# One tile for bank 6 of PSUM in an attention and DFT kernel: value sums and scores share it, and every value product has 17 columns

## The chip, the cores and the metric

The kernel runs on one core of a Trainium2 chip. Its time is device microseconds (us) from the run's own measurement; a kernel's time is the median of several runs. The profile is one further execution with the hardware profiler on; its span goes from the first to the last instruction, and is a little shorter than the time measured for that same execution.

## The reference

Two mixers work on sequences of 2048 rows and 512 columns, and a gate adds them. The first is a Fourier mix, written as products with DFT matrices; the second is softmax attention with 32 heads of 16 columns.

```python
def _A_ref(x, dft_seq_re, dft_seq_im, dft_hid_re, dft_hid_im):
    a = jnp.einsum("bsd,ed->bse", x, dft_hid_re)
    b = jnp.einsum("bsd,ed->bse", x, dft_hid_im)
    return jnp.einsum("ts,bse->bte", dft_seq_re, a) - jnp.einsum("ts,bse->bte", dft_seq_im, b)

def _B_ref(x, wqkv, wo):
    ...
    scores = jnp.einsum("bhqd,bhkd->bhqk", q, k) * scale
    p = _softmax(scores, axis=-1)
    o = jnp.einsum("bhqk,bhkd->bhqd", p, v)
    return (lambda x, *d: x.transpose(*d))(o, 0, 2, 1, 3).reshape(B, S, D) @ wo

g = _sigmoid((x * gate_w).sum(-1, keepdims=True))
return g * a + (1 - g) * b
```

## The kernel before

Everything is written out in the order in which each engine is to run it; no scheduler moves it. The attention goes by pairs of heads (16 pairs), halves of the queries (2) and blocks of 128 keys (16): 512 units in all. For each unit, four score products of 128 keys by 512 queries (line 795, two query blocks, two heads) go to PSUM, ScalarE (ACT in the profile) takes their exponential into an SBUF tile `pt` (line 796), and a value product for each of the four multiplies the exponentials with the values (line 843). Scores need the row maxima first, so each score tile is also computed a first time with queries and keys swapped (line 292, kind "a" below), and VectorE (DVE) takes the maximum of it (line 294). Scores of kind "s" are those of line 795.

A score or maximum product uses 64 of TensorE's 128 rows. Beside it, on the other 64 rows, runs half of a DFT or projection product (line 469). A value product uses all 128 rows and one 32-column quarter of the array; the four of a unit stand in the four quarters and run side by side. Each is one matmul in the program, with single-precision operands; the profile shows it as two matmuls, each with a weight load of its own. So a unit has two groups of four matmuls in the profile.

A value product has 17 stationary columns: 16 value columns and a column of ones, which gives the sum that the softmax divides by. It writes partitions 32j to 32j+16 of bank 6, for j from 0 to 3. The rest of each quarter is never used, but the copies out of the bank take all 128 partitions.

PSUM has eight banks. Scores use banks 0 to 6 by number, the DFT and projection chains use the eighth. Bank 6 is shared: value products add up in it (the tile `acc`), and between two sums it takes scores too. The order of the middle of the kernel is written as strings of slots, played by `segment`. The one that holds most of the time is

```python
FULL = "a5 s4 a2 s0 a3 s6 a5 s4 s1 s0 s2 a6 a3 a4 s5 a1 | |"
```

A letter with a digit is a product of that kind in that bank; each also issues one line-469 matmul on the other half of the rows. A bar is the value products of one unit. The last bar of a segment closes the sum: `evacuate` has ACT copy bank 6 to SBUF (line 822, or line 816 for the first copy of a total), and GpSimd (POOL) adds it to the running total (line 823). So in `FULL` bank 6 goes through: the copy of the last sum, the score `s6`, its exponential on ACT, the maximum product `a6`, its maximum on DVE, the value products of two units, the copy. There are 192 `FULL` segments; 26 `THIN` and 26 `NINE` segments have two bars with other slots between them and use bank 6 for an `s6` alone; with the opening at the start that is 245 sums.

Before the change each use of bank 6 by a score is a tile of its own (`s` or `a`) of a pool with one buffer, and each sum opens with a new tile `acc`. A new tile in that buffer waits for the end of all use of the last. Because the copy reads all 128 partitions of a tile that is new, the first value products of a sum are 32 columns wide (`width`), so that they write each partition of their quarter; the columns past the 17th are values of another head, and what they give is not used.

Of the kernel before, what the change touches and what calls it, by code (L numbers as in the profile page):

```python
# [9 lines left out]
F32 = mybir.dt.float32  # L10
# [5 lines left out]
P = 128  # L16
# [6 lines left out]
NT = S // P  # L23
# [8 lines left out]
def mix_kernel(ctx: ExitStack, tc: tile.TileContext, xa_t, xa, wqkv, w_hid, w_seq, wo, gate_w, out):  # L32
# [5 lines left out]
    nc = tc.nc  # L38
# [29 lines left out]
    psO = Ring(6)  # L68
# [31 lines left out]
    acc = psO.tile([P, 512], F32, "acc")  # L100
# [86 lines left out]
    def bank():  # L187
        nonlocal banks
        banks += 1
        return (psS if banks % 2 else psA).tile([P, 512], F32, name="s" if banks % 2 else "a")  # L190


    with tc.tile_pool(name="qk", bufs=1, reuse_waits="tile") as pool:
# [38 lines left out]
        for tb in range(4):  # L232
# [4 lines left out]
            for c in range(2):  # L237
                if tb == 0 and c == 0:
                    pss = [bank() for _ in range(4)]
                    for kt in range(KT):  # L240
                        x = xab[tb][:, :, :, kt * P:(kt + 1) * P]
# [8 lines left out]
                for ct in range(4):  # L250
                    ps = bank()
# [34 lines left out]
    def a_tile(i, h, ps=None, bank=None):  # L286
        p, j = divmod(i, 64)
        qt, kb = divmod(j, 4)
        if ps is None:
            ps = psA.tile([P, 512], F32, "a", bank)  # L290
        r = slice(64 * h, 64 * h + (64 if p else 48))
        nc.tensor.matmul(ps, qs[p % 2][r, qt * P:(qt + 1) * P], ks[p % 2][r, kb * 512:(kb + 1) * 512],  # L292
                         start=True, stop=True)
        user = nc.vector.tensor_reduce(mx[p % 2][:, h, qt, kb:kb + 1], ps, AX.X, ALU.max)  # L294
        hf = j // 32
        a_left[p, hf] = a_left.get((p, hf), 64) - 1
        if not a_left[p, hf]:
            deferred.extend((partial(m_parts, p, hf), partial(m_rows, p, hf)))
        return user
# [111 lines left out]
    for s in range(8):  # L411
        ps = psS.tile([P, 512], F32, name="s")
# [369 lines left out]
    def scores(u, qb, h, bank=(psS, "s"), number=None):  # L782
        p, r = divmod(u, 32)
        hf, kt = divmod(r, 16)
        q0 = hf * 1024 + qb * 512
        if u >= UNITS - 16:

            blk, kt = divmod(kt, 8)
            q0, kt = 1024 + blk * 512, 2 * kt + qb
        if u not in pts:  # L790
            pts[u] = work.tile([P, 4, 512], F32, name="pt", bufs=4)
        pool, name = bank
        ps = pool.tile([P, 512], F32, name=name) if number is None else pool.tile([P, 512], F32, name, number)
        rr = slice(64 * h, 64 * h + (64 if p else 50))
        nc.tensor.matmul(ps, ks[p % 2][rr, kt * P:(kt + 1) * P], qs[p % 2][rr, q0:q0 + 512], start=True, stop=True)  # L795
        return nc.scalar.activation(pts[u][:, 2 * qb + h], ps, AF.Exp, bias=0.0, scale=DH ** -0.5)  # L796

    def pv_last(u):
        blk, k2 = divmod(u - UNITS + 16, 8)
        pt = pts.pop(u)  # L800
        for j in range(4):
            x, h = divmod(j, 2)
            nc.tensor.matmul(acc[32 * j:32 * j + 17], vt[:, 2 * k2 + x, NP - 1, 16 * h:16 * h + 17], pt[:, j],
                             start=k2 == 0, stop=k2 == 7)
        if blk == 0 and k2 == 7:
            last_pairs.append(LastPair(0, [(psS, "s"), (psA, "a")]))
            last_pairs[0].copy(1)

    part = []

    def evacuate(p, hf, done):

        nonlocal total
        if total is None:
            total = work.tile([P, 512], F32, name="oe", bufs=2)
            nc.scalar.copy(total, acc)
        else:
            if not part:
                two = work.tile([P, 2, 512], F32, name="part", tag="w15")
                part.extend(two[:, i] for i in range(2))  # L820
            part.reverse()
            nc.scalar.copy(part[0], acc)  # L822
            nc.gpsimd.tensor_tensor(total, total, part[0], ALU.add)  # L823
        if done:
            for qb in range(2):
                nc.sync.dma_start(o_d[hf][p, :, qb * 512:(qb + 1) * 512], total[64 * qb:64 * qb + 64])
            total = None

    def pv(u, close=False):
        nonlocal acc  # L830
        if u >= UNITS - 16:
            return pv_last(u)
        p, r = divmod(u, 32)
        hf, kt = divmod(r, 16)
        pt = pts.pop(u)
        begin, done, width = acc is None or kt == 0, kt == NT - 1, 17
        if acc is None:
            acc = psO.tile([P, 512], F32, "acc")
            width = 32
        v = vt.rearrange("p t n d -> p (t n d)")[:, 33 * (NP * kt + p):]  # L840
        for j in range(4):
            h = j % 2
            i = nc.tensor.matmul(acc[32 * j:32 * j + width], v[:, 16 * h:16 * h + width], pt[:, j],  # L843
                                 start=begin, stop=done or close)
        if done or close:
            evacuate(p, hf, done)
            if close:
                acc = None
        return i

    def take(gen, n, whole=True):
# [84 lines left out]
    users, valued, exponentials = [], 0, []  # L936

    def score(kind, h, number=None):
        x = next(streams[h][kind == "a"], None)
        if x:  # L940
            users.append((kind, a_tile(*x, bank=number) if kind == "a" else scores(*x, number=number)))
            if kind == "s":
                exponentials.append(users[-1][1])

    def values(close=False):
        nonlocal valued
        i = pv(valued, close)
        valued += 1
        return i

    def segment(pattern, half, ds, stop):
# [6 lines left out]
        for n, slot in enumerate(pattern.split()):  # L958
# [18 lines left out]
            if first:  # L977

                score(slot, 1 - half, number)
# [12 lines left out]
            if slot != "-" and not first:  # L992
                score(slot[-1] if slot[0] == "+" else slot[0], 1 - half, number)
            if len(slot) == 2 and slot[0] != "+":
                score(slot[1].lower(), half, other)
# [38 lines left out]
    for bank in (*three[:1], *three):  # L1034
        scores(*next(streams[1][0]), bank)
# [8 lines left out]
    for u in range(valued + 2, UNITS, 2):  # L1044
        run_plan(u)
        for i in range(4):
            if i == 2:
                for gen, n in whole[u]:
                    pump(gen, n)
                if u == 506:  # L1050
                    last_pairs[0].turn()
                elif u == 508:
                    last_pairs[0].back()
            for h in range(2):
                scores(u + i // 2, i % 2, h, three[h])
        values()
        values()
    last_pairs[0].products([(psS, "s"), (psA, "a"), (psA, "a"), (psD, "d")], range(4))
    pv(UNITS - 2)
    pv(UNITS - 1)  # L1060
    last_pair(late)

# [35 lines left out]
```

## Time and profile before

| | |
|---|---|
| median of 3 runs | 1665.3 us (1664.87 to 1665.42) |
| the profiled execution's own time | 1664.94 us |
| its span | 1663.0 us |
| mean granted TensorE clock | 0.999 |
| PE (TensorE matmul) busy | 1655.0 us |
| PEld (TensorE weight load) busy | 1008.6 us |
| DVE, ACT, POOL busy | 1382.6, 1266.0, 653.5 us |

A row of the profile that groups instructions reads: line, engine, operation, what it writes and reads, shapes, and count; then the busy time in us, the mean of one in ns, and the engine's idle time just before, with what ended it. A form such as `128*32` is active rows by active columns. Matmuls overlap, so their busy time is a union, and the end of each is modelled. In a timeline a row is a start in us, a length in us, the engine and the instruction.

### The profile page before, as it was taken

To read this page: it belongs to the slowest core of one execution; us is meant where nothing else is said; L and a number is where in the kernel's file an instruction comes from. 1 tells how busy PE (TensorE), PEld (TensorE's weight loads), DVE (VectorE), ACT (ScalarE), POOL (GpSimd) and SP (SyncE) were. 2 spreads that over 40 slices of the span, in tenths; PEclk is the share of its full clock that TensorE was granted. 3 is DMA by queue.
4 is the path that set the end of the run, shared out by engine and by line. 5 is a ranking of instruction groups with operands and counts; after the bars stand their busy time and mean duration, and the time that the engine had idled before them with its cause. 6 is when DMAs were issued, how large, how long until landed. Compare 5 with 4: busy or idle time off the path is not lost.

```text
span 1663.0 us, 34370 instructions
## 1 busy us (share of the span) xinstructions
PE 1655.0 (100%) x13040; PEld 1008.6 (61%) x13040; DVE 1382.6 (83%) x2361; ACT 1266.0 (76%) x2469; POOL 653.5 (39%) x615
## 2 busy tenths in 40 slices
PE   9999999999999999999999999999999999999998
PEld 7888855556566656665666656665566556644443
DVE  5439888888888888888888888888888888899954
ACT  5212388888888888888788888888788878889996
POOL 0202133443434455444343455544444456333330
PEclk9999999999999999999999999999999999999999
DMA  9973610414151343414157534315141535462114
GB/s 295 349 158 120 180 15 9 70 34 85 44 93 47 73 112 81 94 46 79 47 90 254 93 114 96 88 56 90 52 85 59 112 103 122 139 188 40 37 32 140
DMA packets 85245, 167.13 MB, mean 100 GB/s; under 512 B 22461, under 2 KB 22717, under 8 KB 81069
## 3 DMA queue, kind: packets, MB, share of 16 engines
q1 hardware_dynamic: 84648, 164.30, 39.5%
q8 instruction: 102, 1.67, 0.5%
q10 hardware_dynamic: 432, 0.66, 0.1%
q14 instruction: 63, 0.51, 0.1%
HBM read 109.67 MB, written 55.17 MB: 99 GB/s over the span
## 4 chain that ended last, share of the span: by engine, by line
PE 98%; DMA 1%; DVE 0%; POOL 0%; SPq 0%; issue 0%; DVEq 0%; ACT 0%; POOLq 0%; ACTq 0%
PE acc L843 28%; PE d L469 24%; PE a L292 17%; PE s L795 16%; PE s L383 3%; PE s L415 1%; PE d L383 1%; PE a L108 1%; PE s L108 1%; PE s L107 1%; PE a L107 1%; PE a L109 1%; PE s L109 1%; PE a L469 1%; PE s L469 0%; PE s L244 0%
## 5 line engine op out<-in xcount | busy, mean ns | idle before, releaser
L294 DVE TENSOR_REDUCE mx<-a 128x1 f32<-128x512 f32 x2026 | 1260.1, 683 | 172.8 <-PE a L292 144.5
L796 ACT ACTIVATE pt<-s 128x512 f32<-128x512 f32 x2006 | 1021.9, 623 | 33.7 <-PE s L795 17.6
L292 PE MATMUL a<-ks,qs 64*128 64x512 f32 (+1 forms) x2026 | 723.6, 407 | 0.0
L795 PE MATMUL s<-qs,ks 64*128 64x512 f32 (+1 forms) x2006 | 663.9, 395 | 1.0 <-DVE on L736 0.8
L469 PE MATMUL d<-xab,ch 64*128 64x512 f32 x2016 | 644.7, 394 | 0.0
L823 POOL TENSOR_TENSOR oe<-oe,part 128x512 f32<-128x512 f32 x215 | 278.0, 1293 | 660.5 <-ACT part L822 655.5
L292 PEld LDWEIGHTS a<-ks,qs 64*128 64x128 f32 (+1 forms) x2026 | 361.0, 184 | 212.3 <-issue 123.3
L843 PE MATMUL acc<-pt,vt 128*17 128x512 f32 (+1 forms) x3968 | 487.2, 599 | 0.0
L795 PEld LDWEIGHTS s<-qs,ks 64*128 64x128 f32 (+1 forms) x2006 | 361.4, 184 | 71.3 <-ACT pt L796 27.3
L469 PE MATMUL d<-xab,cl 64*128 64x512 f32 x1008 | 397.6, 394 | 0.0
L469 PEld LDWEIGHTS d<-xab,ch 64*128 64x128 f32 x2016 | 366.6, 184 | 28.0
L822 ACT COPY part<-acc 128x512 f32<-128x512 f32 x215 | 126.1, 587 | 187.2 <-PE acc L843 186.2
L843 PEld LDWEIGHTS acc<-pt,vt 128*17 128x17 f32 (+1 forms) x3968 | 92.9, 102 | 218.3 <-issue 138.9
L469 PEld LDWEIGHTS d<-xab,cl 64*128 64x128 f32 x1008 | 185.7, 184 | 14.3
L454 POOL TENSOR_TENSOR cl<-craw,ch 128x512 fp32r<-128x512 f32 x126 | 162.2, 1287 | 10.1
L469 PE MATMUL d<-wre,xab 64*128 64x512 f32 x336 | 90.3, 402 | 0.0
L469 PEld LDWEIGHTS d<-wre,xab 64*128 64x128 f32 x336 | 59.9, 184 | 40.2 <-issue 12.1
L453 POOL CAST ch<-craw 128x512 fp32r<-128x512 f32 x126 | 77.0, 611 | 17.3 <-PE s L795 10.2
L469 PE MATMUL d<-wo_hl,o_hl 64*128 64x512 f32 (+1 forms) x246 | 65.3, 397 | 0.0
L103 ACT CAST hl<-s 128x512 fp32r<-128x512 f32 x28 | 16.1, 587 | 58.4 <-PE s L383 31.3
L469 PEld LDWEIGHTS d<-wo_hl,o_hl 64*128 64x128 f32 (+1 forms) x246 | 44.2, 185 | 16.3 <-ACT pt L796 10.2
L383 PE MATMUL s<-wch,xab 64*128 64x512 f32 x192 | 41.3, 391 | 0.0
(171 smaller groups left out, 992.7 us busy)
## 6 DMA issues: line engine op xcount, KB each, us to landing
craw<-w_seq SPq DMA_DIRECT2D x128, 256.0 KB
qk<-hl SPq DMA_DIRECT2D x32, 512.0 KB
qs<-qk SPq DMA_DIRECT2D x96, 128.0 KB
ks<-qk SPq DMA_DIRECT2D x96, 128.0 KB
b<-hl SPq DMA_DIRECT2D x16, 512.0 KB
xab<-b SPq DMA_DIRECT2D x16, 512.0 KB
o<-oe SPq DMA_DIRECT2D x62, 128.0 KB
oh<-nh SPq DMA_DIRECT2D x12, 512.0 KB
```

The costliest lines, as they stand in the source:

```text
L107: nc.tensor.matmul(ps, sh, mh, start=first, stop=False)
L292: nc.tensor.matmul(ps, qs[p % 2][r, qt * P:(qt + 1) * P], ks[p % 2][r, kb * 512:(kb + 1) * 512], start=True, stop=True)
L294: user = nc.vector.tensor_reduce(mx[p % 2][:, h, qt, kb:kb + 1], ps, AX.X, ALU.max)
L383: i = nc.tensor.matmul(ps, st[r], mv[r], start=not half and not j, stop=half == 1 and j == 11)
L453: nc.gpsimd.tensor_copy(h1, raw)
L454: nc.gpsimd.tensor_tensor(l1, raw, h1.bitcast(F32), ALU.subtract)
L469: i = nc.tensor.matmul(self.ps, st[r], mv[r], start=not self.begun, stop=stop)
L795: nc.tensor.matmul(ps, ks[p % 2][rr, kt * P:(kt + 1) * P], qs[p % 2][rr, q0:q0 + 512], start=True, stop=True)
L796: return nc.scalar.activation(pts[u][:, 2 * qb + h], ps, AF.Exp, bias=0.0, scale=DH ** -0.5)
L822: nc.scalar.copy(part[0], acc)
L823: nc.gpsimd.tensor_tensor(total, total, part[0], ALU.add)
L843: i = nc.tensor.matmul(acc[32 * j:32 * j + width], v[:, 16 * h:16 * h + width], pt[:, j], start=begin, stop=done or close)
```

## The change

The tile `acc`, made once at the start, is kept for the whole kernel. A score or maximum in bank 6 writes to `acc` itself and no longer takes a tile from the pool. A sum opens by a flag (`closed`) in place of a new tile, and its first products have 17 columns as all others do. Partitions 17 to 31 of each quarter then hold what the last score in the bank left there; the copy and the running total carry it, and nothing reads it.

```diff
@@ scores
-        ps = pool.tile([P, 512], F32, name=name) if number is None else pool.tile([P, 512], F32, name, number)
+        if number == 6:
+            ps = acc
+        else:
+            ps = pool.tile([P, 512], F32, name=name) if number is None else pool.tile([P, 512], F32, name, number)
@@
-    part = []
+    part, closed = [], False
@@ pv
-        nonlocal acc
+        nonlocal closed
...
-        begin, done, width = acc is None or kt == 0, kt == NT - 1, 17
-        if acc is None:
-            acc = psO.tile([P, 512], F32, "acc")
-            width = 32
+        begin, done = closed or kt == 0, kt == NT - 1
+        closed = False
...
-            i = nc.tensor.matmul(acc[32 * j:32 * j + width], v[:, 16 * h:16 * h + width], pt[:, j],
+            i = nc.tensor.matmul(acc[32 * j:32 * j + 17], v[:, 16 * h:16 * h + 17], pt[:, j],
                                  start=begin, stop=done or close)
         if done or close:
             evacuate(p, hf, done)
-            if close:
-                acc = None
+            closed = close
@@ score
-            users.append((kind, a_tile(*x, bank=number) if kind == "a" else scores(*x, number=number)))
+            users.append((kind, a_tile(*x, acc if number == 6 else None, number) if kind == "a" else scores(*x, number=number)))
```

No engine gets an instruction more or less among those that compute or move data, and none changes its place. Two things differ: widths on TensorE, and waits on ScalarE. The end of a `FULL` segment on TensorE, before (the names are the tiles that a matmul writes and reads; the size is what it writes; the brackets name the engine whose count it waits for):

```order
L795 MATMUL s<-qs_972,ks_974 128x512 [waits DVE_49]
L469 MATMUL d<-xab_205,ch 128x512
L292 MATMUL a<-ks_975,qs_973 128x512 [waits Activation_49]
L843 MATMUL acc<-pt,vt 32x512 [waits DVE_49]
L843 MATMUL acc<-pt,vt 32x512 x3
L843 MATMUL acc<-pt,vt 17x512 x3
L843 MATMUL acc<-pt,vt 17x512 [waits Activation_49]
L292 MATMUL a<-ks_975,qs_973 128x512 [waits Activation_49]
```

and the same place in the changed kernel:

```order
L798 MATMUL s<-qs_972,ks_974 128x512 [waits DVE_49]
L469 MATMUL d<-xab_204,ch 128x512
L292 MATMUL a<-ks_975,qs_973 128x512 [waits Activation_49]
L844 MATMUL acc<-pt,vt 17x512 [waits DVE_49]
L844 MATMUL acc<-pt,vt 17x512 x6
L844 MATMUL acc<-pt,vt 17x512 [waits Activation_49]
L292 MATMUL a<-ks_975,qs_973 128x512 [waits Activation_49]
```

The four opening products have 17 columns in place of 32, and the waits are the same: the first still waits for the maximum that DVE takes from bank 6, the last for an exponential. The same place on ScalarE, where a segment's copy stands among the exponentials, before:

```order
L796 ACTIVATE pt<-s 128x512 [waits PE_49,Activation_49]
L796 ACTIVATE pt<-s 128x512 [waits PE_49]
L822 COPY part<-acc 128x512 [waits PE_49,Pool_49]
L796 ACTIVATE pt<-s 128x512 [waits PE_49] x4
L796 ACTIVATE pt<-s 128x512 [waits PE_49,Activation_49]
```

and in the changed kernel:

```order
L799 ACTIVATE pt<-s 128x512 [waits PE_49,Activation_49]
L799 ACTIVATE pt<-s 128x512 [waits PE_49]
L825 COPY part<-acc 128x512 [waits DVE_49,PE_49,Pool_49]
L799 ACTIVATE pt<-s 128x512 [waits PE_49] x2
L799 ACTIVATE pt<-acc 128x512 [waits PE_49]
L799 ACTIVATE pt<-s 128x512 [waits PE_49]
```

The copy has one wait more, for DVE: the tile that it reads is now the one from which DVE took the maximum, where before it was a newer tile. This holds for the 192 copies of the `FULL` segments, 168 on line 822 and 24 on line 816. The exponential of `s6` now reads `acc`.

## The prediction

> **What bounds the kernel now.** I read the page's totals first, then its chain of waits, then the groups of the value products by form.
>
> ```profile
> span 1663.0 us, 34370 instructions
> PE 1655.0 (100%) x13040; PEld 1008.6 (61%) x13040; DVE 1382.6 (83%) x2361; ACT 1266.0 (76%) x2469; POOL 653.5 (39%) x615
> PE 98%; DMA 1%; DVE 0%; POOL 0%; SPq 0%; issue 0%; DVEq 0%; ACT 0%; POOLq 0%; ACTq 0%
> PE acc L843 28%; PE d L469 24%; PE a L292 17%; PE s L795 16%; PE s L383 3%; PE s L415 1%; PE d L383 1%; PE a L108 1%; PE s L108 1%; PE s L107 1%; PE a L107 1%; PE a L109 1%; PE s L109 1%; PE a L469 1%; PE s L469 0%; PE s L244 0%
> ```
>
> TensorE is 98% of the chain, and the value products of line 843 are its largest part, 28%. So what lengthens or shortens TensorE's own stream counts in full; what happens on ACT or DVE counts only once it is late enough to hold a matmul.
>
> **What the change does to TensorE.** The value products stand in the profile in two forms.
>
> ```profile
> L843 PE MATMUL acc<-pt,vt 128*17 128x512 f32 x2008 | 261.4, 593 | 0.0
> L843 PE MATMUL acc<-pt,vt 128*32 128x512 f32 x1960 | 261.1, 605 | 0.0
> L843 PEld LDWEIGHTS acc<-pt,vt 128*17 128x17 f32 x2008 | 54.3, 97 | 138.9 <-issue 138.9
> L843 PEld LDWEIGHTS acc<-pt,vt 128*32 128x32 f32 x1960 | 38.6, 108 | 79.4 <-DVE mx L294 61.5 <-ACT pt L796 17.6 <-PE a L795 0.3
> ```
>
> An opening is four products and eight matmuls of the profile, so 1960 matmuls of 32 columns are 245 openings. The wide form has a mean 12 ns above the narrow one, and its weight load a mean 11 ns above. Which of the eight are longer, and whether the next start moves with them, is seen in short windows around one group of four each. In time order: the first four of a wide opening, its second four, and the first four after a narrow one's start elsewhere.
>
> ```profile
> L843 PE MATMUL acc<-pt,vt 128*32 128x512 f32 x4 | 0.6, 617 | 0.0
> ...
> L843 PE MATMUL acc<-pt,vt 128*32 128x512 f32 x4 | 0.6, 592 | 0.0
> ...
> L843 PE MATMUL acc<-pt,vt 128*17 128x512 f32 x4 | 0.6, 604 | 0.0
> ```
>
> The second four take 592 ns though they are just as wide: their loads are done while the first four run. The first four have nothing of their kind to hide behind, and there the width shows: 617 ns with 32 columns, 604 with 17. The starts of the weight loads say the same. Each later group's load starts as the group before it begins to run. First a sum that opens wide (line 843), then units that open narrow (line 803, the last pair of heads):
>
> ```profile
> 800.55 0.16 PEld L843 LDWEIGHTS acc<-pt,vt 128*32 128x32 f32 x8 [0.30 <-DVE mx L294]
> 801.01 0.13 PEld L843 LDWEIGHTS acc<-pt,vt 128*17 128x17 f32 x4 [0.30 <-issue]
> 801.44 0.12 PEld L843 LDWEIGHTS acc<-pt,vt 128*17 128x17 f32 x4 [0.30 <-issue]
> ...
> 1626.01 0.13 PEld L803 LDWEIGHTS acc<-pt,vt 128*17 128x17 f32 x8 [0.30 <-issue]
> 1626.45 0.12 PEld L803 LDWEIGHTS acc<-pt,vt 128*17 128x17 f32 x4 [0.31 <-issue]
> 1626.88 0.12 PEld L803 LDWEIGHTS acc<-pt,vt 128*17 128x17 f32 x4 [0.31 <-issue]
> ```
>
> From the first to the second load it is 0.46 us wide and 0.44 narrow, and 0.43 between later groups in both. So the start of the following group moves by the 13 ns (rounded to 20 here), and with it everything behind it on TensorE. The change takes these 13 ns from each of 245 openings; 617 and 604 are rounded, so it is 12 to 14 ns, and 245 x 0.012 to 245 x 0.014 is 2.9 to 3.4 us. I take 3.1, a little below the middle of the two, since the forms' means give 12. Bounds: nothing, if the width is hidden; and 245 x 4 x 0.011 = 10.8 us, if each of the four loads of a group gave its 11 ns one after another. Eight loads of 108 ns end within 0.16 us in the row at 800.55, so they run side by side, and the low price is far nearer.
>
> The idle 0.30 us ahead of a wide opening is put down to DVE's maximum. It stays, but costs nothing: the narrow opening at 1626.01 waits for no maximum and has the same 0.30. It is the time in which TensorE finishes the half-row products before it can take full-row ones.
>
> The Trainium skill, "TensorE: Matmul & The Clock Gate", section "Architectural detail: the array is 16× 32×32, not 1× 128×128", says that a matmul can begin before its weight load is complete, as a part of the array can run while others still load. By that rule the width of an opening would hide behind its own first matmuls and the sum would be zero; it is the second case below. The rows of 617 and 604 ns speak against it for the first group of a sum.
>
> **What the change does to ACT.** The copies of the 192 `FULL` segments get a wait for DVE. Here is one segment boundary on ACT, DVE and the weight loads, and how long a wait instruction of ACT takes with one condition (line 822) and with two (line 816):
>
> ```profile
> 807.61 0.61 PE L843 MATMUL acc<-pt,vt 128*17 128x512 f32 x4
> 808.37 0.59 ACT L822 COPY part<-acc 128x512 f32<-128x512 f32 x1 [1.14 <-PE acc L843]
> 808.93 2.07 ACT L796 ACTIVATE pt<-s 128x512 f32<-128x512 f32 x4
> 802.94 5.04 DVE L294 TENSOR_REDUCE mx<-a 128x1 f32<-128x512 f32 x8 [0.71 <-PE a L292]
> 808.69 1.29 DVE L294 TENSOR_REDUCE mx<-a 128x1 f32<-128x512 f32 x2 [0.70 <-PE a L292]
> 809.19 0.18 PEld L795 LDWEIGHTS s<-qs,ks 64*128 64x128 f32 x1
> L822 ACTq EVENT_SEMAPHORE  x211: 17/17/17, 211.5 to 1614.1; - x106
> L816 ACTq EVENT_SEMAPHORE  x30: 17/38/38, 204.5 to 1575.6; - x30
> ```
>
> The awaited maximum of bank 6 is one of the eight that end by 802.94 + 5.04 = 807.98, and the value products, which the copy waits for anyway, could not have opened without it. They end at 808.22. So the new wait never ends last. Its price is at most the step from 17 to 38 ns, 21 ns, at the copy's start. Behind the copy ACT has the exponentials, and TensorE has `s6`, the third score of the next segment, which writes to bank 6: its weight load starts at 809.19, the copy ends at 808.96. The margin is 0.23 us, and 21 ns are covered by it. ACT itself sat idle 1.14 us before the copy, DVE 0.70 in each segment, so a small delay of the exponentials behind it is made good within the segment. Without that cover the 21 ns would cost 192 x 0.021 = 4.0 us. I take nothing.
>
> The rest is free of cost: no instruction is moved, the copies read stale partitions of the same size, `s6` and `a6` write the same bank, and the waits on TensorE name the same instructions.
>
> **The sum.** Against the profiled execution, 1664.94 us by its own clock, 1.94 above its span: 1664.94 - 3.1 = 1661.8. The median shown is 0.36 higher, so 1665.3 - 3.1 = 1662.2 us.
>
> **The rivals.**
>
> The width is hidden, or the gain is taken up by waits behind it: **no change, 1665.3 us**. For it: 592 ns in the second group, whatever its width; and TensorE does wait for others now and then.
>
> ```profile
> PEld a L292 <- DVE mx L294: 23.1, 28, 0.9
> PEld s L795 <- ACT pt L796: 27.3, 38, 0.8
> PEld d L469 <- ACT pt L796: 21.3, 25, 0.9
> ```
>
> Against it: these are 91 waits in 245 sums, and most sums have none that a matmul could be held by.
>
> The copy holds TensorE: **slower**. The mechanism is the longer wait ahead of the copy; the place is the load of `s6` in each `FULL` segment; it decides once the copy is more than 0.23 us later than now. If every copy then held `s6` back by a whole two-condition wait, 38 ns, that is 192 x 0.038 = 7.3 us lost against 3.1 won, +4.2, and 1669.5 us. For it: one more condition on the very instruction behind which bank 6 comes free. Against: 0.23 us of margin against 21 ns.
>
> The four loads count one by one: **faster, 1665.3 - 10.8 = 1654.5 us**. For it: the mean load is 11 ns shorter. Against: the spacing of 0.46 and 0.44 us above.
>
> That the edit changes nothing at all, since the value products stay as wide, is excluded by the rows shown with the change.
>
> **How the numbers follow.** The forecast has 0.75, no change 0.12, slower by the copy 0.08, the large gain 0.05. What a measurement of this kernel can tell from no change is about 0.2%, 3.3 us: the three runs shown spread by 0.55 us. The forecast of 3.1 us lies just on the near side of that bound. Its own spread, from 2.9 to 3.4 by the rows and, as an estimate from the three runs shown, half a microsecond more on either side for the measurement, puts 0.27 of its 0.75 beyond it. Faster by over 0.2%: 0.27 + 0.05 = 0.32. Within 0.2%: 0.48 + 0.12 = 0.60. Slower: 0.08. The range reaches from 1660.6, the forecast less 1.6, to 1665.4, so that it holds the case of no change; it leaves out the last two cases.
>
> **What would show it.** In the changed kernel there is one form of value product, 128*17, with 3968 matmuls; the first four of a sum take 604 ns and not 617, and the load of the next group follows after 0.44 us. PE busy falls by about 3 us, as does the span. ACT's copies carry a wait instruction of 38 ns, start no more than 21 ns later behind the last value matmul, and the load of `s6` still starts after the copy's end with 0.2 us to spare. The forecast is wrong if the first four still take 617 ns, if the load of `s6` in a `FULL` segment has idle time that is put down to ACT, or if waits on DVE or ACT grow by as much as the openings shrink.

## The result, and the profile after

| | before | changed |
|---|---|---|
| median of 18 runs | 1665.26 us (1664.09 to 1666.32) | 1661.88 us (1661.19 to 1663.07) |
| ratio to before | 1 | 0.9981, 95% interval 0.9974 to 0.9987 |
| span of the profiled execution | 1663.0 us | 1659.9 us |
| PE busy | 1655.0 us | 1652.6 us |

The changed kernel is faster by 3.4 us, 0.19%; the two sets of runs do not overlap. By the bound of the prediction this is within 0.2%, and its interval reaches across that bound on one side and is clear of no change on the other. The profiled spans differ by 3.1 us.

The page of the changed kernel, its totals and its chain of waits:

```profile
span 1659.9 us, 34392 instructions
PE 1652.6 (100%) x13040; PEld 1011.9 (61%) x13040; DVE 1383.2 (83%) x2361; ACT 1267.3 (76%) x2469; POOL 653.5 (39%) x615
...
PE 98%; DMA 1%; DVE 0%; POOL 0%; SPq 0%; issue 0%; DVEq 0%; ACT 0%; POOLq 0%; ACTq 0%
```

TensorE is still 98% of the chain. The 22 instructions more are wait instructions on ACT. PE's busy time fell by 2.4 us. The value products, grouped by form, and one window on the first four matmuls of an opening:

```profile
L844 PE MATMUL acc<-pt,vt 128*17 128x512 f32 x3968 | 484.1, 596 | 0.0
L844 PEld LDWEIGHTS acc<-pt,vt 128*17 128x17 f32 x3968 | 87.9, 96 | 219.9 <-issue 140.5 <-DVE mx L294 61.8 <-ACT pt L799 17.6
...
L844 PE MATMUL acc<-pt,vt 128*17 128x512 f32 x4 | 0.6, 603 | 0.0
```

One form is left, and an opening's first group has gone from 617 ns to 603 (604 in most openings). The idle time put down to DVE is 61.8 us where it was 61.5: it did not shrink with the openings, and it cost nothing before either. Another wait did change its name. Waits of the weight loads of line 292, before and then changed (total us, times, longest; `issue` is idle time for which the profile shows no cause):

```profile
PEld a L292 <- issue: 123.3, 145, 0.9
PEld a L292 <- ACT pt L796: 12.8, 15, 0.9
...
PEld a L292 <- issue: 99.5, 117, 0.9
PEld a L292 <- ACT pt L799: 36.9, 44, 0.9
```

Waits on ACT grown by more than the openings shrink were named as a sign against the forecast. But the two rows add up to 136.1 and 136.4 us, and in the `FULL` segments the step from the last group of value matmuls to the next matmul is 522 ns in the median of both kernels. So some of the same idle time is put down to another cause, and no matmul is held longer. The timeline of a `FULL` boundary of the changed kernel on weight loads and on ACT (start, length, engine, instruction):

```profile
821.97 0.13 PEld L844 LDWEIGHTS acc<-pt,vt 128*17 128x17 f32 x8 [0.35 <-DVE mx L294]
822.42 0.12 PEld L844 LDWEIGHTS acc<-pt,vt 128*17 128x17 f32 x4 [0.31 <-issue]
822.84 0.12 PEld L844 LDWEIGHTS acc<-pt,vt 128*17 128x17 f32 x4 [0.31 <-issue]
...
824.85 0.18 PEld L798 LDWEIGHTS acc<-qs,ks 64*128 64x128 f32 x1
...
824.02 0.59 ACT L825 COPY part<-acc 128x512 f32<-128x512 f32 x1 [1.17 <-issue]
824.59 1.09 ACT L799 ACTIVATE pt<-s 128x512 f32<-128x512 f32 x2
L825 ACTq EVENT_SEMAPHORE  x211: 17/2080/2120, 211.5 to 1611.6; - x106
```

The load of `s6`, which now reads as a score in `acc`, starts at 824.85, and the copy ends at 824.61: 0.24 us to spare, where it was 0.23. The last row is ACT's wait ahead of the copy. Its median went from 17 ns to 2080. That is no new wait: the instruction had one condition, TensorE's, and stood on ACT until it held; now it has two, starts once the first of them is met, and the time of the second is inside its length. In the median it starts 32 ns after DVE's maximum of bank 6 has ended.

For the comparisons below I cut each trace at the first value matmul of each stage, from the start of the first matmul to the end of the last. In us:

```
                    to the    THIN     FULL     NINE    the     sum
                    values    (26)     (192)    (26)    end
before              203.7     152.7    1103.1   142.1   54.5    1656.1
changed             203.7     152.3    1101.0   141.9   54.0    1653.0
wide opening        204.0     152.6    1103.5   142.4   54.9    1657.3
all wide            204.3     152.9    1103.0   142.6   54.6    1657.3
four columns        203.6     151.9    1098.7   141.4   54.4    1650.0
bars together       204.5     165.3    1102.0   156.7   55.0    1683.4
small copy ahead    204.4     152.5    1101.1   145.6   55.1    1658.6
copy twice          203.8     161.0    1176.8   154.1   54.5    1750.1
```

Between before and changed, `FULL` gives 2.1 us of the 3.1 (192 openings of 13 ns would be 2.5), `THIN` 0.3 (26 openings: 0.3), `NINE` 0.2 (0.3). The last stage gives 0.5 where it has no opening to give it; stages move by that much from one execution to the next, as the rows of the other kernels show.

A finer count leaves out what else happens in a stage. TensorE has 308 runs of value matmuls, each of two or four groups of four. From the start of a run's first group to the start of its second:

```
                 median in FULL, ns    sum over the 308 runs, us
before                  453                    138.8
changed                 441                    135.8
wide opening            453                    138.9
all wide                453                    139.6
four columns            430                    132.4
```

These are starts, not modelled ends. The changed kernel gains 3.0 us in this one place, 12 ns for an opening; the steps into a run and out of it have the same medians in both kernels, 323 and 522 ns in `FULL`.

### The profile page after: what moved, and what is told of

It reads as the page before. It is cut to its first block, busy times and chain, and to the rows that moved or that the text cites. A ratio compares the mean times of both kernels' runs of the same rounds, so it can differ in the third digit from the quotient of the medians.

```text
span 1659.9 us, 34392 instructions
## 1 busy us (share of the span) xinstructions
PE 1652.6 (100%) x13040; PEld 1011.9 (61%) x13040; DVE 1383.2 (83%) x2361; ACT 1267.3 (76%) x2469; POOL 653.5 (39%) x615
## 4 chain that ended last, share of the span: by engine, by line
PE 98%; DMA 1%; DVE 0%; POOL 0%; SPq 0%; issue 0%; DVEq 0%; ACT 0%; POOLq 0%; ACTq 0%
PE acc L844 28%; PE d L469 26%; PE a L292 16%; PE s L798 12%; PE s L383 3%; PE acc L798 3%; PE s L415 1%; PE d L383 1%; PE acc L292 1%; PE s L107 1%; PE s L109 1%; PE a L109 1%; PE a L107 1%; PE a L108 1%; PE s L108 1%; PE a L469 1%
## 5 line engine op out<-in xcount | busy, mean ns | idle before, releaser
L294 DVE TENSOR_REDUCE mx<-a 128x1 f32<-128x512 f32 x1834 | 1144.2, 683 | 155.0 <-PE a L292 145.9
L799 ACT ACTIVATE pt<-s 128x512 f32<-128x512 f32 x1762 | 933.5, 626 | 33.2 <-PE s L798 17.2
L798 PE MATMUL s<-qs,ks 64*128 64x512 f32 (+1 forms) x1762 | 575.4, 396 | 0.5 <-DVE on L736 0.3
L844 PE MATMUL acc<-pt,vt 128*17 128x512 f32 x3968 | 484.1, 596 | 0.0
L798 PEld LDWEIGHTS s<-qs,ks 64*128 64x128 f32 (+1 forms) x1762 | 317.0, 185 | 59.1 <-ACT pt L799 27.8
L844 PEld LDWEIGHTS acc<-pt,vt 128*17 128x17 f32 x3968 | 87.9, 96 | 219.9 <-issue 140.5
L294 DVE TENSOR_REDUCE mx<-acc 128x1 f32<-128x512 f32 x214 | 147.8, 690 | 14.9 <-PE acc L292 0.2
L799 ACT ACTIVATE pt<-acc 128x512 f32<-128x512 f32 x244 | 148.1, 607 | 0.0
L798 PE MATMUL acc<-qs,ks 64*128 64x512 f32 (+1 forms) x244 | 95.4, 391 | 0.0
L292 PE MATMUL acc<-ks,qs 64*128 64x512 f32 (+1 forms) x214 | 83.4, 390 | 0.0
```

What stands on the lines that cost most here:

```text
L844: i = nc.tensor.matmul(acc[32 * j:32 * j + 17], v[:, 16 * h:16 * h + 17], pt[:, j], start=begin, stop=done or close)
```

## The experiments

**One part undone: wide openings on the one tile.**

```diff
+        width = 32 if closed else 17
         closed = False
...
-            i = nc.tensor.matmul(acc[32 * j:32 * j + 17], v[:, 16 * h:16 * h + 17], pt[:, j],
+            i = nc.tensor.matmul(acc[32 * j:32 * j + width], v[:, 16 * h:16 * h + width], pt[:, j],
```

> The changed kernel with one part undone: bank 6 is still one tile for the whole kernel, and the copies still wait for DVE too, but the first value products of a sum have 32 columns again. Theory (the weight load of an opening is exposed, and its length goes with the columns): all of the gain is gone, 1665.3 us, 3.4 above the changed kernel; the first four matmuls of a sum take 617 ns again, with 0.45 us to the next group. Rival (the gain comes from the one tile and its waits): the gain stays, 1661.9 us.

Measured: 1665.95 us, ratio to before 1.0002 (0.9993 to 1.0011). The gain is gone. First groups stand at 617 ns again, and the second group follows after 453 ns. The forms are those of before to the nanosecond:

```profile
L845 PE MATMUL acc<-pt,vt 128*17 128x512 f32 x2008 | 261.4, 593 | 0.0
L845 PE MATMUL acc<-pt,vt 128*32 128x512 f32 x1960 | 261.1, 605 | 0.0
```

So the one tile and its waits are worth nothing that can be measured (the interval reaches from 1.2 us won to 1.8 lost), and the starts put all of the 3 us on the 15 columns. The other half of this test, narrow openings with a new tile for each sum, wasn't tried: there the copy would read partitions of the tile that nothing has written.

**The width in every product.**

```diff
+        width = 17 if p == NP - 1 and kt == NT - 1 else 32
...
+            i = nc.tensor.matmul(acc[32 * j:32 * j + width], v[:, 16 * h:16 * h + width], pt[:, j],
```

> The changed kernel with 32 columns in every value product of the main part, not in the openings alone (one product of the last pair of heads stays at 17). Theory (only a group that begins a run of value products on TensorE is exposed): 245 openings as before the change, and the 52 second units of THIN and NINE segments, which also begin a run: 297 x 13 ns = 3.9 us above the changed kernel, 1665.8 us; the second unit of a FULL segment is not lengthened. Rival (each unit's first group costs the 13 ns): about 490 units x 13 ns = 6.4 us, 1668.3 us. Rival (each of the eight matmuls' loads counts): over 1680 us.

Measured: 1666.16 us, ratio 1.0004 (0.9995 to 1.0013); against the changed kernel's 0.9981 that is 0.23%, 3.8 us, where 3.9 was expected for exposed groups alone.

```profile
L845 PE MATMUL acc<-pt,vt 128*32 128x512 f32 x3960 | 487.1, 600 | 0.0
```

Twice as many wide matmuls have a lower mean, 600 ns against 605, since those that were added stand mostly at 592: a second unit in a `FULL` segment loads its weights while the first unit's matmuls run. From wide openings to all wide the stages show 0.3 us in `THIN` and 0.2 in `NINE`, where 26 second units each begin a run (26 x 13 ns = 0.3), and none in `FULL`, where 192 second units would have shown 2.5. The stages move by as much by themselves, but the starts say the same: the runs of all wide take 3.7 us more than those of the changed kernel, and 0.7 more than those of wide openings, none of it in `FULL`. Both rivals fall.

**Fewer columns still.**

```diff
-            i = nc.tensor.matmul(acc[32 * j:32 * j + 17], v[:, 16 * h:16 * h + 17], pt[:, j],
+            i = nc.tensor.matmul(acc[32 * j:32 * j + 4], v[:, 16 * h:16 * h + 4], pt[:, j],
```

> The changed kernel with 4 columns in every value product but those of the last pair's second half: 13 of 17 columns of the value product, the column of the softmax sums among them, are left out. Theory (the exposed load goes with the columns, 13 ns for 15 of them): 13 columns less give 11 ns at each of some 300 runs of value products, 3.4 us, 1658.5 us, and the first four matmuls of a run take 593 ns, close to the 592 of a covered group. Rival (a floor at or above 17 columns): 1661.9 us and 604 ns.

Measured: 1659.27 us, ratio 0.9961 (0.9949 to 0.9974), 0.20% or 3.3 us below the changed kernel's ratio. (By the medians alone it is 2.6 us.)

```profile
L844 PE MATMUL acc<-pt,vt 128*4 128x512 f32 x3968 | 480.7, 592 | 0.0
```

With 4 columns the mean of all is 592 ns, that of a covered group: next to nothing of the load is left to see. First groups stand at 593 (592 to 594), 604 and 617 ns for 4, 17 and 32 columns, (617 - 593) / 28 = 0.86 ns for a column. The starts, which are not modelled, give 430, 441 and 453 ns to the second group, (453 - 430) / 28 = 0.82 ns. Between two later groups it is 429, so at 4 columns 1 ns is left to win, and there is no floor above that. The Trainium skill, "TensorE: Matmul & The Clock Gate", section "LDWEIGHTS (loading the stationary operand)", gives a load's time as its columns over 1.2, 0.83 ns for each; the slope here agrees.

**The two bars of THIN and NINE side by side.** An attempt to win more: TensorE pays for each step from half-row products to full-row ones and back, so one such step less in 52 segments.

```diff
-            "a2 s4 a1 s3 a0 s6 a5 s2 a4 s3S1 | a5A0 s3 a4 s2 |")
+            "a2 s4 a1 s3 a0 s6 a5 s2 a4 s3S1 a5A0 s3 a4 s2 | |")
```

(and likewise in the other three strings)

> The changed kernel with the two units of value products of each THIN and NINE segment side by side at the segment's end, as FULL has them, in place of other products between them. Same work, other order. Theory (each change between half-row and full-row products costs TensorE a fixed time, and the second one of a segment goes): a run of eight matmuls costs 323 + 441 + 542 ns against 230 for a step of a pair, plus 100 ns in the second step behind it, and a run of sixteen 859 ns more than a run of eight: 2 x 1176 against 2035, 0.32 us less in each of 52 segments, 16 us, 1646 us. Rival (VectorE sets the pace of these segments: 92% busy in the NINE ones, and 2 us without maxima to take leave it idle): no gain or a loss, 1662 to 1675 us.

Measured: 1692.18 us, ratio 1.0158 (1.0144 to 1.0172), a loss of 30 us against the changed kernel, worse than the rival's range. The rows of TensorE in this kernel have idle time (the last column) where the kernel before had none on line 292 and 1.0 us on its line of scores:

```profile
L292 PE MATMUL a<-ks,qs 64*128 64x512 f32 (+1 forms) x1834 | 686.8, 410 | 6.4 <-DVE mx L294 6.4
L798 PE MATMUL s<-qs,ks 64*128 64x512 f32 (+1 forms) x1762 | 582.0, 398 | 16.9 <-ACT pt L799 14.2 <-DVE on L736 0.9 <-DVE yp L668 0.6
```

6.4 + 16.9 = 23.3 us of idle TensorE, ended by ACT's exponentials (14.2) and DVE's maxima (6.4) for the most part; `THIN` lost 13.0 us and `NINE` 14.8. Value products are what TensorE does while the other two engines empty the score banks. Put at the end, they leave a run of scores that comes faster than DVE and ACT take them. The theory's term may well be there, but it is smaller than this loss, and the run does not show it apart.

**The copy held back a little, and a lot.** These two test the statement that the copies have room. First one small copy more ahead of each:

```diff
+            nc.scalar.copy(few[:, :1], acc[:, :1])
             nc.scalar.copy(part[0], acc)
```

> The changed kernel with one small copy more on ACT, of one column of bank 6, ahead of each copy that closes a sum (215 of them). Theory (the copy has 0.24 us to spare before the load of s6 of the next segment): the copy is 0.1 to 0.25 us later, the spare time shrinks to near nothing, and the kernel's time moves by less than 0.2%, 1661.9 us. Rival (the copy is on TensorE's path): 0.1 to 0.25 us in each of 192 FULL segments, 19 to 48 us, 1681 to 1710 us.

Measured: 1667.76 us, ratio 1.0011 (1.0002 to 1.0020): 5.0 us above the changed kernel by the ratios, 5.9 by the medians, more than the 3.3 that the theory allowed and far less than the rival's 19 us. The stages tell where: `FULL` took 1101.05 us against 1101.04, `NINE` 3.7 us more, the end 1.1, the part before the values 0.6. So the statement held in `FULL`, but the run was a weak test of it: the two copies overlap on ACT, and the large one ended only 19 ns later in the median. What it shows instead is that `NINE` has less room on ACT. In the changed kernel ACT is 91% busy there, against 82% in `FULL` and 87% in `THIN`; with the small copy the weight loads of scores in `NINE` wait 28.5 us for exponentials, where the changed kernel has 23.9. A closing copy in `NINE`, with the small one ahead of it:

```profile
1484.00 0.16 ACT L825 COPY few<-acc 128x1 f32<-128x1 f32 x1 [0.28 <-PE acc L845]
1484.05 0.59 ACT L826 COPY part<-acc 128x512 f32<-128x512 f32 x1
```

The idle time ahead of the copy, 0.28 us here and 1.17 in the `FULL` row above, does not by itself tell which stage loses: in `THIN` it is 0.06 us in the median, and `THIN` lost 0.2 us.

Then the whole copy twice:

```diff
+            nc.scalar.copy(part[0], acc)
             nc.scalar.copy(part[0], acc)
```

> The changed kernel with each copy that closes a sum made twice. Theory (the copy has 0.24 us to spare, and what is beyond it holds TensorE): the second copy ends some 0.56 us later, 0.32 us beyond the spare time, which in 192 FULL segments is up to 61 us, 1723 us, less what TensorE has queued ahead of s6. Rival (ACT is nowhere near TensorE's path): 1661.9 us. Rival (ACT becomes the bound in all segments): 215 x 0.56 = 120 us, 1782 us.

Measured: 1760.10 us, ratio 1.0567 (1.0551 to 1.0583), 98 us above the changed kernel; 75.7 us of it in `FULL`, 0.39 us for each segment, and the rest in the other two. Here the load of `s6` waits for the copy: the third row of the weight loads' waits (total us, times, longest) is in neither of the two kernels' lists:

```profile
PEld a L292 <- ACT pt L799: 194.9, 517, 0.9
PEld s L798 <- ACT pt L799: 103.9, 417, 0.9
PEld acc L798 <- ACT part L826: 50.3, 213, 0.5
```

From the starts in the trace, medians over the `FULL` segments and counted from the modelled end of the last value matmul: the last copy ends 1341 ns later, in place of 723, and the load of `s6` starts at 1392, in place of 966. So bank 6 opens for TensorE 51 ns after the copy's end, and the changed kernel has 966 - 723 - 51 = 192 ns of true margin, a little less than the 0.24 us between the two rows. The theory's mechanism holds in `FULL`. Its price of 61 us was too low: it left out those 51 ns and took 0.56 us for a copy that costs ACT 0.62. With both, the load comes 1392 - 966 = 426 ns later, which in 192 segments is up to 82 us, and 75.7 were lost. It also priced nothing for `THIN` and `NINE`, which lost 8.7 and 12.2 us. There and in `FULL` exponentials come later too: the first two rows stood at 36.9 and 27.8 us in the changed kernel. The rival with ACT as the bound falls, as ACT is 84% busy in `FULL` even here.

## Why the prediction was right

**The bound.** TensorE's stream was named as what sets the end. The gain in TensorE's openings came out of the time nearly whole: 3.0 us by the starts, 3.1 in the span, 3.4 in the medians.

**The size.** 245 openings of 12 to 14 ns, 3.1 us taken. Undone, extended to every product and made smaller, the width gave what exposed groups alone give, and nothing else did. The 13 ns came from lengths with modelled ends; by the starts an opening gives 12, at the lower end of the range. That the means of the two forms give 12 as well is chance: such a mean depends on how many covered matmuls are in each form. The second experiment shows it, with 600 in place of 605 ns for matmuls of the same width. One row was read loosely: the eight loads at 800.55 are those of the first two groups, and the load at 801.01 is the third group's, which starts as the second group begins to run. The spacing is still that of the first two groups, so the argument stands. Both groups of an opening have the same width in every kernel here; the first is named as the exposed one because the second group's loads end 0.30 us before its matmuls start.

**The waits on ACT, costed at nothing.** Right in the sum, wrong in the details. A wait instruction of 38 ns and a start at most 21 ns later were named; the instruction takes 2080 ns in the median, and the copy starts earlier, 137 ns behind the modelled end of the last value matmul and not 148. Wide openings on the one tile have 137 too, so it is the waits and not the width. It is worth nothing to the time, as the copy had room on both sides.

**The rival of no change** (a load that hides behind its own first matmuls) and **the large gain** (four loads counted one by one) both fall with the experiments on width: 12 ns show for 15 columns, not none and not 44. Of the rule of the Trainium skill, "TensorE: Matmul & The Clock Gate", section "Architectural detail: the array is 16× 32×32, not 1× 128×128", that a matmul can begin before its load is complete, this case shows that it does not hide the width: an exposed first group gets longer at 4, 17 and 32 columns, with 430, 441 and 453 ns to the second group.

**The rival of a slower kernel** through the copy needed a delay of over 0.23 us. The point from which it decides is real, and at 192 ns; the change moved the copy 11 ns the other way.

**The chances.** The forecast lay just under the 0.2% bound and the result does too. Which side of it a repeat would fall on isn't settled by the interval.

## What to carry to other kernels

In this kernel a weight load was hidden behind a group of matmuls that use the array in the same way: 429 ns from group to group, at 17 columns and at 32. Where a run of matmuls came after another use of the array's rows, its first load was exposed, and each column from 4 to 32 cost some 0.8 ns. Why the first load finds no cover there, no run tested. So look at the first group of each run in short windows, since means over a form mix exposed and covered ones, and take the starts, since the ends are modelled. And where matmuls of one kind give other engines time to catch up, putting them together to save such beginnings can cost far more than it saves.

## What the runs showed of the hardware that was not expected

A wait instruction on ACT with two conditions, of which the one for TensorE is met last, let the copy behind it start 11 ns sooner than one with that condition alone: 137 against 148 ns behind the modelled end of the last value matmul, in the medians over the 168 `FULL` copies of line 822 (825 in the changed kernel). Its length in the profile then holds the waiting time (2080 ns in the median, against 17), so a long wait instruction is no sign of a longer wait. The 24 `FULL` copies of line 816 (819) start sooner still, after 93 ns in both kernels: there the copy itself waits for TensorE, and the wait instruction ahead of it has the other conditions. Why the starts differ was not tested.
